# K transposed in pairs of chunks, w_down on the attention rows, masks on VectorE: a decode block on one core

## The chip, the cores and the metric

One core of one Trainium2 chip. The metric is the device time of one execution in microseconds (us); smaller is better. The profile's engines are named in full here: TensorE (PE, its weight loads PEld), VectorE (DVE), ScalarE (ACT), GpSimd (POOL), and SP, which issues most of the DMAs.

## What is computed

One decode step of a transformer block for one token, in bfloat16: a layer norm, grouped-query attention over a cache of 65,536 positions (32 query heads, 4 KV heads, width 128), the residual, a second layer norm, and a GeGLU feed-forward of width 3584 with its residual.

```python
h  = x + A(layernorm(x))            # x: [1, 1, 1024]
h2 = h + B(layernorm(h))

A: q = x @ wq                       # wq [1024, 4096], 8 query heads share a KV head
   p = softmax((q . k) * 128**-0.5) # k_cache, v_cache [4, 65536, 128]
   o = p @ v;  o @ wo               # wo [4096, 1024]
B: (gelu(x @ w_gate) * (x @ w_up)) @ w_down   # [1024, 3584] twice, [3584, 1024]
```

K and V are 67 MB each, wq and wo 8.4 MB each, the three feed-forward matrices 7.3 MB each: 173 MB that are read once.

## The kernel before

**The ring.** All large loads go through one SBUF ring of four slots of 4 MB (32 KB a partition), handed out in order by `chunk`; a load takes one or two slots, and SP issues it once the work on what lay there is done. SP's order is wq (2 slots), then K and V, wo, w_gate, w_up, w_down. The K loads are 4 MB each, two chunks of 64 positions a partition; there are 8 chunks and 4 such loads to a KV head. V of the first KV head comes in loads of 4, 4 and 8 MB, later ones in loads of 8 MB. In the first KV head K loads follow one another; from the second on, two K loads alternate with V of the head before.

**Scores.** `k_chunk` (L253) makes per chunk four VectorE transposes of 32x32 blocks, 128x1024 f32 words each, into `kt` (six buffers), and after each of them four matmuls of 512 columns into one score bank of three (L268). `score_chunk` transposes the bank back (L278) and takes maxima (L279). The queries stand in `qs`, spread over partitions by 16 small POOL copies a KV head (L226). `softmax_head` brings the maxima together and runs the exponentials on ScalarE.

**Values.** `v_chunk` multiplies with V in four column quadrants of TensorE into `acc` (L317). After a head ScalarE copies `acc` to SBUF (L326), four f32 matmuls with `sel` pick out each head's own columns (L329), and VectorE copies them into `o_raw` (L331). At the end the heads are divided by their sums and transposed (L349 to L372).

**After the attention.** wo (L410) puts the attention output on two rows of each half of `at_ps`, which `fold_columns` (L418, L420) turns into columns; VectorE adds x (L427), the second layer norm follows, and w_gate and w_up (L446, through L186 and L199).

**w_down.** Its last row of each partition's share is loaded early into `c_sb` by 12 small DMAs (L400). The rest comes as 4 MB (16 rows a partition), then 7, 3 and 1 rows. Each row is eight matmuls of 128 columns (L489), one for each eighth of the output, onto single partitions of two banks, `d_ps` and `d_odd`. The residual h is put there beforehand as `hb`, by eight POOL operations (L473) and eight matmuls (L475). Two casts (L510, L511) and the store (L512) end the kernel.

**Order.** The program is written in the order of the code, but a scheduler sets each engine's order ahead of time by when it takes operands to be ready, and adds the waits; an engine then runs its list in order. On VectorE the list has the eight transposes of a K load, then both of its chunks' score transposes and maxima, although `k_chunk` and `score_chunk` alternate in the code.

Of the kernel before, what the change touches and what calls it, by code (L numbers as in the profile page):

```python
# [9 lines left out]
ALU = mybir.AluOpType  # L10
# [7 lines left out]
def kernel(  # L18
# [47 lines left out]
    ktpool = ctx.enter_context(tc.tile_pool(name="ktpool", bufs=6))  # L66
# [3 lines left out]
    ps_m = ctx.enter_context(tc.tile_pool(name="ps_m", bufs=3, space=PSUM))  # L70
    ps_qk = ctx.enter_context(tc.tile_pool(name="ps_qk", bufs=3, space=PSUM))
    ps_acc = ctx.enter_context(tc.tile_pool(name="ps_acc", bufs=2, space=PSUM))
# [17 lines left out]
    wq_v = A_wq.rearrange("(p t c) n -> t p c n", t=DS, c=C4)  # L90
    assert C4 * HD == CW and DS * C4 == DC
    XU = 32
    XV = P // XU
    x_in = const.tile([XU, XV, DC], BF16, name="x_in")
    nc.scalar.dma_start(out=x_in[:], in_=A_x[0, 0].rearrange("(u v j) -> u v j", u=XU, j=DC))
    wq_tiles = []
    for t in range(DS):
# [16 lines left out]
    xsel = ktpool.tile([XU, XV, P], BF16, name="xsel", tag="kt")  # L114
    nc.gpsimd.memset(xsel[:], 0.0)
    nc.gpsimd.affine_select(out=xsel[:], in_=xsel[:], compare_op=ALU.not_equal, fill=1.0, base=0,
                            pattern=[[-1, XV], [1, P]], channel_multiplier=-XV)


    esel = const.tile([P, 4, P], BF16, name="esel")  # L120
    for q in range(4):
        for i in range(NI):
# [9 lines left out]
    sel16 = const.tile([P, 16], F32, name="sel16")  # L132
    nc.vector.tensor_tensor(out=sel16[:], in0=sel[:, 0:16], in1=sel[:, 16:32], op=ALU.add)
    o_of = const.tile([P, 8], F32, name="o_of")
    nc.vector.memset(o_of[:], 1.0)
    nc.gpsimd.affine_select(out=o_of[:], in_=o_of[:], compare_op=ALU.is_ge, fill=0.0, base=0,
                            pattern=[[-16, 8]], channel_multiplier=1)
    nc.gpsimd.affine_select(out=o_of[:], in_=o_of[:], compare_op=ALU.is_ge, fill=0.0, base=15,
                            pattern=[[16, 8]], channel_multiplier=-1)
# [34 lines left out]
    for v in range(XV):  # L174
        nc.tensor.matmul(x_ps[:], lhsT=xsel[:, v, :], rhs=x_in[:, v, :], start=(v == 0), stop=(v == XV - 1))
# [43 lines left out]
    def make_qs(g):  # L219

        qs = qspool.tile([P, 4, NS, P], BF16, name="qs", tag="qs")
        nc.gpsimd.memset(qs[:], 0.0)  # L222
        for i in range(NI):
            rows = slice(SQ * i, SQ * (i + 1))
            for s in range(NS):
                nc.gpsimd.tensor_copy(out=qs[rows, :, s, SQ * i + s:SQ * (i + 1):NS], in_=qsel[rows, :, g * rep:(g + 1) * rep])  # L226
        return qs
# [3 lines left out]
    o_raw = const.tile([P, Hq], F32, name="o_raw")  # L231
# [6 lines left out]
    def load(src, ci, name, blocks):  # L238

        si = ci  # L240
        for b in blocks:
            if si < DCH * b:
                break
            si -= DCH * b
        if si == 0:
            tv = chunk(b).rearrange("p (n d) -> p n d", d=Dh)
            nc.sync.dma_start(out=tv, in_=src[:, ci * CH:(ci + DCH * b) * CH, :])
            loaded[name] = tv
        return loaded[name][:, si * CH:(si + 1) * CH, :]

    def k_chunk(g, ci):

        st = kst.setdefault(g, {})  # L253
        if ci == 0:
            st["qs"] = make_qs(g)
            st["mx"] = small.tile([P, rep, NCH], F32, name="mx", tag="mx")
            st["sc"] = []
        k_sb = load(k_v[g], ci, "k_sb", [1] * (NCH // DCH))
        k32 = k_sb.rearrange("p n d -> p (n d)").bitcast(F32)
        W = NN * Dh // 2  # L260
        qk = ps_qk.tile([P, NN * SQ], F32, name="qk_ps", tag="qk")
        for s in range(NS):
            kt = ktpool.tile([P, W], F32, name="kt", tag="kt")
            nc.vector.transpose(out=kt[:], in_=k32[:, s * W:(s + 1) * W])  # L264
            mv = kt[:].bitcast(BF16).rearrange("p (n j b t) -> p n j b t", n=NN, j=2, t=2)
            for jt in range(4):
                J, t = divmod(jt, 2)
                nc.tensor.matmul(qk[:], lhsT=st["qs"][:, jt, s, :], rhs=mv[:, :, J, :, t],  # L268
                                 start=(s == 0 and jt == 0), stop=(s == NS - 1 and jt == 3))
        st[("qk", ci)] = qk  # L270
# [37 lines left out]
    def v_chunk(g, ci):  # L308
        st = vst[g]
        v_sb = load(v_v[g], ci, "v_sb", [1, 1, 2] if g == 0 else [2, 2])  # L310
        if ci == 0:
            st["acc"] = ps_acc.tile([P, NS * Dh], F32, name="acc_ps", tag="acc")
        acc = st["acc"]
        pt = st["pts"][ci // CPH]
        for n in range(NN):
            c = n % 4
            nc.tensor.matmul(acc[32 * c:32 * c + 32, :], lhsT=pt[:, ci % CPH, n, :, :].rearrange("p h s -> p (h s)"),  # L317
                             rhs=v_sb[:, n:CH:NN, :],
                             start=(ci == 0 and n < 4), stop=(ci == NCH - 1 and n >= NN - 4),
                             tile_position=(0, 32 * c))  # L320
        if ci == NCH - 1:
            assert NH == 2
            heads = slice(g * rep, (g + 1) * rep)
            nc.vector.tensor_tensor(out=lsum[:, heads], in0=st["lpart"][:, 0, :], in1=st["lpart"][:, 1, :], op=ALU.add)  # L324
            acc_sb = small.tile([P, NS * Dh], F32, name="acc_sb", tag="accsb")
            nc.scalar.copy(out=acc_sb[:], in_=acc[:])  # L326
            o_ps = misc([P, rep], F32, "o_ps")
            for t in range(NS):
                nc.tensor.matmul(o_ps[:], lhsT=acc_sb[:, t * Dh:(t + 1) * Dh], rhs=sel[:, t:SQ:NS],  # L329
                                 start=(t == 0), stop=(t == NS - 1))  # L330
            nc.vector.tensor_copy(out=o_raw[:, heads], in_=o_ps[:])  # L331
            vst.pop(g)

    VB = 2 * DCH
    for g in range(Hkv):
        for ci in range(NCH):
            k_chunk(g, ci)
            if ci >= 1:
                score_chunk(g, ci - 1)
            if ci == NCH - 1:  # L340
                score_chunk(g, ci)
                softmax_head(g)
            if g >= 1 and ci % VB == VB - 1:
                for vi in range(ci - VB + 1, ci + 1):
                    v_chunk(g - 1, vi)
    for ci in range(NCH):
        v_chunk(Hkv - 1, ci)
    l_ps = misc([P, Hq], F32, "l_ps")
    nc.tensor.matmul(l_ps[:], lhsT=ones_f[:], rhs=lsum[:], start=True, stop=True)  # L349
    rl = const.tile([P, Hq], F32, name="rl")  # L350
    nc.vector.reciprocal(out=rl[:], in_=l_ps[:])
    oT_all = const.tile([P, Hq], BF16, name="oT_all")
    nc.vector.tensor_tensor(out=oT_all[:], in0=o_raw[:], in1=rl[:], op=ALU.mult)


    WN = CW // D
    assert Hq % WN == 0 and Hq * OQ == P and Dh == OQ * Hq
    oh_ps = misc([Hq, Dh], BF16, "oh_ps")
    nc.tensor.transpose(out=oh_ps[:], in_=oT_all[:], identity=ident_bf[:])
    o_sb = small.tile([Hq, Dh], BF16, name="o_sb", tag="o_sb")  # L360
    nc.vector.tensor_copy(out=o_sb[:], in_=oh_ps[:])
# [44 lines left out]
    c_dma()  # L406
    for c in range(Hq):
        for s in range(DS):
            q = 2 * (c % 2) + s
            nc.tensor.matmul(at_ps[32 * q:32 * q + 32, :], lhsT=o2z[:, c, :], rhs=wv[:, c, :].rearrange("k (p s c) -> k s p c", s=DS, c=C4)[:, s],  # L410
                             start=(c < 2), stop=(c >= Hq - 2), tile_position=(0, 32 * q))
# [14 lines left out]
    h_col = const.tile([P, DC], F32, name="h_col")  # L426
    nc.vector.tensor_tensor(out=h_col[:], in0=hc_ps[:], in1=x_col[:], op=ALU.add)  # L427


    hz = xz  # L430
    layernorm_cols(h_col[:], hz[:, :, 0], "ln2")
# [11 lines left out]
    def ffn_in(wmat, name):  # L443
        banks = bank_pair(name + "_w", FW)
        wv = chunk(2)[:, 0:DC * F].rearrange("p (c n) -> p c n", c=DC)
        nc.sync.dma_start(out=wv, in_=wmat.rearrange("(p c) n -> p c n", p=P))  # L446
# [23 lines left out]
    hb = ktpool.tile([P, DC, P], F32, name="hb", tag="kt")  # L470
    nc.gpsimd.memset(hb[:], 0.0)
    for r in range(OR):
        nc.gpsimd.tensor_scalar(out=hb[:, :, orow[r]], in0=h_col[:], scalar1=o_of[:, r:r + 1], scalar2=None, op0=ALU.mult)  # L473
    for j in range(DC):
        nc.tensor.matmul(d_ps[:, j:OB:DC], lhsT=hb[:, j, :], rhs=sel16[:], start=False, stop=False, skip_group_check=True)  # L475
    d_odd = ps_acc.tile([P, OB], F32, name="d_odd", tag="acc")
    nc.vector.tensor_copy(out=d_odd[64:P, :], in_=d_ps[64:P, :])
# [6 lines left out]


# [11 lines left out]
    for f0, nr, pieces in ((0, FA, (FA,)), (P * FA, FB, (FB - 5, 3, 1))):  # L497
# [3 lines left out]
        for sz in pieces:  # L501
            nc.sync.dma_start(out=wv[:, e0:e0 + sz, :], in_=wsrc[:, e0:e0 + sz, :])
            for e in range(e0, e0 + sz):
                down(actz[:, f0 // P + e, :], wv[:, e, :])
            e0 += sz
        if f0 == 0:
            for r in range(4):
                down(cz[:, r, :], c_sb[:, r, :])
# [34 lines left out]
```

## Time and profile before

| | |
|---|---|
| median of 3 runs | 410.55 us (410.39 to 410.86) |
| span of the profiled execution | 408.8 us (its device time isn't printed apart) |
| DMA | 173.26 MB in 5144 packets, 424 GB/s over the span |
| TensorE busy | 228.8 us, 1623 matmuls and as many weight loads |
| VectorE busy | 205.1 us, of them 146.2 in L264's 128 transposes |
| ScalarE, GpSimd busy | 36.6 and 43.5 us |

The span runs from the first to the last instruction. In the rows of tenths each digit is a fortieth of the span, about 10.2 us. In a timeline a line has start, length, engine, line, operation, output and inputs, the count, and in brackets how long the engine had been idle before and what ended that. In the chain of work that ended last each line is a start, a length and what the end was waiting for in that time; "issue" is time in which nothing visible was waited for.

### The profile page before, as it was taken

The page shows a single profiled execution, that of the slowest core. Times are in us where ns is not written, and L with a number is a line of the kernel's source. Part 1 is how long each engine was busy: PE and PEld are TensorE (multiplying, and loading weights), DVE is VectorE, ACT ScalarE, POOL GpSimd, SP SyncE. Part 2 cuts the span into 40 slices and gives each one's busy share as a digit, 9 for nine tenths or more (in the row PEclk, how much of TensorE's full clock was granted, in tenths as well). Part 3 has the DMA queues.
Part 4 walks back from the last instruction along what each step waited for, and adds up shares of the span by engine and source line. Part 5 has one row for each costly group of instructions (what it writes and reads, how often), then busy time and mean ns, then how long its engine had stood idle before and what let it go on. Part 6 is the DMA issues. An engine that isn't in the chain of part 4 may idle for free.

```text
span 408.8 us, 3981 instructions
## 1 busy us (share of the span) xinstructions
PE 228.8 (56%) x1623; PEld 99.0 (24%) x1623; DVE 205.1 (50%) x263; ACT 36.6 (9%) x136; POOL 43.5 (11%) x150
## 2 busy tenths in 40 slices
PE   1337677688388367844765575576351425275045
PEld 1112222133133132311222222222120113143024
DVE  2118999999299239905980696089500001012010
ACT  1000000070000520000008000000340000000000
POOL 8123000300000400000002400000400100002000
PEclk9966989988888668868996689669885656566688
DMA  8999999999999999999999999999999999999995
GB/s 359 410 462 406 442 430 418 449 415 452 417 457 430 402 444 458 423 410 428 472 417 420 418 478 394 428 462 430 436 418 449 430 442 425 427 432 423 416 410 212
DMA packets 5144, 173.26 MB, mean 424 GB/s; under 512 B 643, under 2 KB 647, under 8 KB 1031
## 3 DMA queue, kind: packets, MB, share of 16 engines
q1 hardware_dynamic: 5079, 173.02, 98.4%
q8 instruction: 12, 0.20, 0.2%
q14 instruction: 5, 0.04, 0.0%
q10 hardware_dynamic: 48, 0.00, 0.0%
HBM read 173.02 MB, written 0.00 MB: 423 GB/s over the span
## 4 chain that ended last, share of the span: by engine, by line
DMA 68%; DVE 22%; PE 5%; issue 4%; SPq 0%; ACT 0%
DMA ring<-in_A_k_cache_dram 42%; DVE kt L264 19%; DMA ring<-in_A_wo_dram 8%; DMA ring<-in_B_w_up_dram 7%; DMA ring<-in_A_v_cache_dram 7%; DMA ring<-in_B_w_down_dram 4%; PE qk_ps L268 2%; PE at_ps L410 2%; PE acc_ps L317 1%; DVE sc L278 1%; DVE mx L279 1%; SPq L100 0%; PE mxT_ps L286 0%; PE d_ps L489 0%; DVE gm L288 0%
## 5 line engine op out<-in xcount | busy, mean ns | idle before, releaser
L268 PE MATMUL qk_ps<-kt,qs 128*128 128x512 bf16 x512 | 141.0, 426 | 59.8 <-DVE kt L264 46.2
L264 DVE STREAM_TRANSPOSE kt<-ring 128x1024 f32<-128x1024 f32 x128 | 146.2, 1208 | 45.4 <-DMA ring<-in_A_k_cache_dram 45.4
L268 PEld LDWEIGHTS <-qs 128*128 128x128 bf16 x512 | 53.7, 105 | 143.8 <-issue 95.1
L317 PE MATMUL acc_ps<-ring,pt 128*32 128x512 bf16 x512 | 44.7, 526 | 50.6 <-DMA ring<-in_A_v_cache_dram 50.6
L301 ACT ACTIVATE pt<-sc,nbias 128x256 bf16<-128x256 f32 x64 | 31.5, 494 | 261.9 <-DVE nbias L294 261.9
L317 PEld LDWEIGHTS <-pt 128*32 128x32 bf16 x512 | 18.4, 127 | 75.2 <-issue 51.8
L331 DVE COPY o_raw<-o_ps 128x8 f32<-128x8 f32 x4 | 0.7, 167 | 48.1 <-PE o_ps L329 48.1
L278 DVE STREAM_TRANSPOSE sc<-qk_ps 128x512 f32<-128x512 f32 x32 | 22.1, 692 | 1.0 <-PE qk_ps L268 1.0
L279 DVE TENSOR_REDUCE mx<-sc 128x8 f32<-128x512 f32 x32 | 22.0, 688 | 1.1
L222 POOL MEMSET qs<- 128x2048 bf16 x4 | 7.2, 1802 | 94.8 <-PE qk_ps L268 94.8
L186 PEld LDWEIGHTS <-xz 128*32 128x32 bf16 x192 | 6.8, 124 | 33.0 <-issue 16.1
L226 POOL COPY qs<-qsel 32x32 bf16<-32x32 bf16 x64 | 11.2, 247 | 16.6 <-DVE qsel L217 15.9
L324 DVE TENSOR_TENSOR lsum<-lpart 128x8 f32<-128x8 f32 x4 | 0.7, 164 | 24.2 <-ACT pt L301 24.2
L186 PE MATMUL qw_ps<-ring,xz 128*32 128x512 bf16 x64 | 7.2, 625 | 9.4 <-DMA ring<-in_A_wq_dram 9.4
L410 PE MATMUL at_ps<-ring,o2z 128*32 128x512 bf16 x64 | 6.6, 594 | 10.4 <-DMA ring<-in_A_wo_dram 10.4
L301 ACT ACTIVATION_READ_ACCUMULATOR pt<-sc,nbias 128x1 f32 x64 | 12.0, 187 | 0.0
L186 PE MATMUL u_ps_w<-ring,xz 128*32 128x512 bf16 (+1 forms) x64 | 4.5, 450 | 10.7 <-DMA ring<-in_B_w_up_dram 10.7
L427 DVE TENSOR_TENSOR h_col<-hc_ps,x_col 128x8 f32<-128x8 f32 x1 | 0.2, 166 | 19.5 <-PE hc_ps L420 19.5
L199 DVE STREAM_TRANSPOSE u_ps_r<-u_ps_w 128x512 f32<-128x512 f32 (+1 forms) x2 | 1.2, 629 | 14.1 <-PE u_ps_w L186 14.1
L199 DVE STREAM_TRANSPOSE q_r<-qw_ps 128x512 f32<-128x512 f32 x2 | 1.3, 696 | 13.6 <-PE qw_ps L186 13.6
L489 PE MATMUL d_ps<-ring,actz 128*32 128x128 bf16 x108 | 5.0, 263 | 5.6 <-DMA ring<-in_B_w_down_dram 5.5
L380 POOL MEMSET cz<- 128x256 bf16 x1 | 0.3, 311 | 72.6 <-PE qk_ps L268 72.6
(104 smaller groups left out, 92.0 us busy)
## 6 DMA issues: line engine op xcount, KB each, us to landing
ring<-in_A_k_cache_dram SPq DMA_DIRECT2D x16, 4096.0 KB
ring<-in_A_wq_dram SPq DMA_DIRECT2D x2, 4096.0 KB
ring<-in_A_v_cache_dram SPq DMA_DIRECT2D x2, 4096.0 KB
ring<-in_B_w_gate_dram SPq DMA_DIRECT2D x1, 7168.0 KB
ring<-in_B_w_up_dram SPq DMA_DIRECT2D x1, 7168.0 KB
ring<-in_B_w_down_dram SPq DMA_DIRECT2D x1, 4096.0 KB
ring<-in_B_w_down_dram SPq DMA_DIRECT2D x1, 1792.0 KB
ring<-in_B_w_down_dram SPq DMA_DIRECT2D x1, 768.0 KB
```

What stands on the lines that cost most here:

```text
L186: nc.tensor.matmul(banks[t // 4][32 * q:32 * q + 32, :], lhsT=rows_z[:, ci, :], rhs=w, start=first, stop=last, tile_position=(0, 32 * q))
L199: nc.vector.transpose(out=r[:, o:o + n].rearrange("p (e j) -> p e j", j=32) if sizes else r[:, o:o + n], in_=src)
L222: nc.gpsimd.memset(qs[:], 0.0)
L226: nc.gpsimd.tensor_copy(out=qs[rows, :, s, SQ * i + s:SQ * (i + 1):NS], in_=qsel[rows, :, g * rep:(g + 1) * rep])
L264: nc.vector.transpose(out=kt[:], in_=k32[:, s * W:(s + 1) * W])
L268: nc.tensor.matmul(qk[:], lhsT=st["qs"][:, jt, s, :], rhs=mv[:, :, J, :, t], start=(s == 0 and jt == 0), stop=(s == NS - 1 and jt == 3))
L278: nc.vector.transpose(out=sc.rearrange("p n h s -> p (n h s)"), in_=qk[:])
L279: nc.vector.tensor_reduce(out=st["mx"][:, :, ci], in_=sc.rearrange("p n h s -> p h n s"), axis=AX.XY, op=ALU.max)
L301: nc.scalar.activation(out=pt[:].rearrange("p c n h s -> p (c n) h s")[:, :, r, :], in_=sc[:].rearrange("p c n h s -> p (c n) h s")[:, :, ...
L317: nc.tensor.matmul(acc[32 * c:32 * c + 32, :], lhsT=pt[:, ci % CPH, n, :, :].rearrange("p h s -> p (h s)"), rhs=v_sb[:, n:CH:NN, :], start ...
L410: nc.tensor.matmul(at_ps[32 * q:32 * q + 32, :], lhsT=o2z[:, c, :], rhs=wv[:, c, :].rearrange("k (p s c) -> k s p c", s=DS, c=C4)[:, s], s ...
L489: nc.tensor.matmul((d_ps, d_odd)[q // 2][32 * q:32 * q + 32, :], lhsT=a_row[:, AZ - m:AZ - m + 32], rhs=w_row[:, j * OB:(j + 1) * OB], sta ...
```

## The change

- **K in pairs.** `k_pair` replaces `k_chunk`: four transposes of 128x2048 words cover both chunks of a load; after each, eight matmuls alternate between the two chunks' score banks, two consecutive ones with the same weights. `kt` has three buffers of twice the size. A chunk's positions are laid out accordingly in `v_chunk`. The score banks stay three.
- **Queries.** Four larger POOL copies a KV head in place of 16.
- **Heads.** After a KV head VectorE multiplies `acc` by a mask `smask` into SBUF, and one f32 matmul of 512 columns with `hsel` adds the result into an `o_ps` bank that is kept for all heads (one bank is taken from the small results). `o_raw`, its copies and the transpose at the end go; a reduction and a scaling remain.
- **x and the layouts.** x is loaded as two rows and turned into columns by four matmuls; wq, w_gate and w_up are read with a matching order of rows (w_gate and w_up as two runs a partition). The output columns of wo are read in plain order.
- **Residual.** Two matmuls put x on the attention rows of `at_ps` before wo; the add of L427 and all of `hb` go.
- **w_down.** `at_ps` is kept. Block 0, the c rows and the first piece of block 1 (now 6 rows; then 4 and 1) are two matmuls of 512 columns a row, onto the same rows of `at_ps`. Then `fold_rows` copies `at_ps` on ScalarE and adds it with eight f32 matmuls of 128 columns into `d_ps` and `d_odd`. The last five rows go as before.

```diff
...
-    ktpool = ctx.enter_context(tc.tile_pool(name="ktpool", bufs=6))
+    ktpool = ctx.enter_context(tc.tile_pool(name="ktpool", bufs=3))
...
-    ps_m = ctx.enter_context(tc.tile_pool(name="ps_m", bufs=3, space=PSUM))
+    ps_m = ctx.enter_context(tc.tile_pool(name="ps_m", bufs=2, space=PSUM))
     ps_qk = ctx.enter_context(tc.tile_pool(name="ps_qk", bufs=3, space=PSUM))
+    ps_o = ctx.enter_context(tc.tile_pool(name="ps_o", bufs=1, space=PSUM))
...
-            for s in range(NS):
-                nc.gpsimd.tensor_copy(out=qs[rows, :, s, SQ * i + s:SQ * (i + 1):NS], in_=qsel[rows, :, g * rep:(g + 1) * rep])
+            nc.gpsimd.tensor_copy(out=qd[rows, :, :, SQ * i:SQ * (i + 1):NS],
+                                  in_=qsel[rows, :, g * rep:(g + 1) * rep].unsqueeze(2).to_broadcast([SQ, 4, NS, rep]))
...
-        W = NN * Dh // 2
-        qk = ps_qk.tile([P, NN * SQ], F32, name="qk_ps", tag="qk")
+        W = DCH * NN * Dh // 2
+        qks = [ps_qk.tile([P, NN * SQ], F32, name="qk_ps", tag="qk") for _ in range(DCH)]
         for s in range(NS):
             kt = ktpool.tile([P, W], F32, name="kt", tag="kt")
             nc.vector.transpose(out=kt[:], in_=k32[:, s * W:(s + 1) * W])
...
             for jt in range(4):
                 J, t = divmod(jt, 2)
-                nc.tensor.matmul(qk[:], lhsT=st["qs"][:, jt, s, :], rhs=mv[:, :, J, :, t],
-                                 start=(s == 0 and jt == 0), stop=(s == NS - 1 and jt == 3))
+                for c in range(DCH):
+                    nc.tensor.matmul(qks[c][:], lhsT=st["qs"][:, jt, s * P:(s + 1) * P], rhs=mv[:, c, :, J, :, t],
+                                     start=(s == 0 and jt == 0), stop=(s == NS - 1 and jt == 3))
...
-            nc.scalar.copy(out=acc_sb[:], in_=acc[:])
...
+            nc.vector.tensor_tensor(out=acc_sb[:], in0=acc[:].rearrange("p (s d) -> p s d", d=Dh),
+                                    in1=smask[:].unsqueeze(2).to_broadcast([P, NS, Dh]), op=ALU.mult)
+            nc.tensor.matmul(o_ps[:], lhsT=hsel[:, Hq - rep - g * rep:2 * Hq - rep - g * rep],
+                             rhs=acc_sb[:].rearrange("p s d -> p (s d)"), start=(g == 0), stop=(g == Hkv - 1))
...
-        for ci in range(NCH):
-            k_chunk(g, ci)
-            if ci >= 1:
-                score_chunk(g, ci - 1)
...
+        for cp in range(NCP):
+            k_pair(g, cp)
+            if cp >= 1:
+                for ci in range((cp - 1) * DCH, cp * DCH):
+                    score_chunk(g, ci)
...
+    for s in range(DS):
+        nc.tensor.matmul(at_ps[32 * s:32 * s + 32, :], lhsT=ident_bf[0:DS, s:s + 32], rhs=x_in[:], start=True, stop=False,
+                         tile_position=(0, 32 * s))
...
-        nc.sync.dma_start(out=wv, in_=wmat.rearrange("(p c) n -> p c n", p=P))
+        nc.sync.dma_start(out=wv.rearrange("p (s c) n -> p s c n", s=DS), in_=wmat.rearrange("(s p c) n -> p s c n", s=DS, c=C4))
...
-    hb = ktpool.tile([P, DC, P], F32, name="hb", tag="kt")
-    nc.gpsimd.memset(hb[:], 0.0)
...
+    fz = qspool.tile([P, DS, 2 * AZ + 1], F32, name="fz", tag="qs")
+    nc.gpsimd.memset(fz[:], 0.0)
+    nc.gpsimd.tensor_copy(out=fz[:, :, AZ], in_=sel2[:])
+
+    def down_wide(a_row, w_row, i):
+        for s in range(DS):
+            q = 2 * (i % 2) + s
+            nc.tensor.matmul(at_ps[32 * q:32 * q + 32, :], lhsT=a_row[:, AZ:AZ + 32], rhs=w_row[:, s * NB:(s + 1) * NB],
+                             start=False, stop=False, skip_group_check=True, tile_position=(0, 32 * q))
+
+    def fold_rows():
+        r = ktpool.tile([P, NB], F32, name="d_w", tag="kt")
+        nc.scalar.copy(out=r[:], in_=at_ps[:])
+        for j in (0, 4, 1, 5, 2, 6, 3, 7):
+            q, m = divmod(orow[j], 32)
+            s, b = divmod(j, OR // DS)
+            nc.tensor.matmul((d_ps, d_odd)[q // 2][32 * q:32 * q + 32, :], lhsT=fz[:, s, AZ - m:AZ - m + 32], rhs=r[:, b * OB:(b + 1) * OB],
+                             start=False, stop=False, skip_group_check=True, tile_position=(0, 32 * q))
...
-    for f0, nr, pieces in ((0, FA, (FA,)), (P * FA, FB, (FB - 5, 3, 1))):
+    for f0, nr, pieces in ((0, FA, (FA,)), (P * FA, FB, (FB - 6, 4, 1))):
...
+                if i == 0:
+                    down_wide(actz[:, f0 // P + e, :], wv[:, e, :], e)
+                else:
+                    down(actz[:, f0 // P + e, :], wv[:, e, :])
...
+            elif i == 0:
+                fold_rows()
...
```

## The prediction

> **What bounds the kernel now.** I read the slices of the span first, then the DMA queues, the chain that ended last, and the timelines of SP, VectorE and TensorE around the places where the chain touches DMA.
>
> ```profile
> DVE  2118999999299239905980696089500001012010
> ...
> DMA  8999999999999999999999999999999999999995
> GB/s 359 410 462 406 442 430 418 449 415 452 417 457 430 402 444 458 423 410 428 472 417 420 418 478 394 428 462 430 436 418 449 430 442 425 427 432 423 416 410 212
> ...
> q1 hardware_dynamic: 5079, 173.02, 98.4%
> q8 instruction: 12, 0.20, 0.2%
> ...
> DMA 68%; DVE 22%; PE 5%; issue 4%; SPq 0%; ACT 0%
> ```
>
> The reader is to see that the DMA row is full from the second slice to the last but one, and that one queue accounts for 98.4% of the 16 engines' span. The chain's 22% of VectorE look like a second bound, but during them DMA is full too: the chain follows a slot that was freed early. The packet records of the trace say it more sharply: a 32,768-byte packet takes 1213 ns on its engine from the first weight load to the last K load, 16 engines x 27.0 GB/s = 432 GB/s, and the next packet starts as the last ends. So what matters is (1) whether the queue ever runs dry, (2) the bytes and packets, (3) what follows the last landing.
>
> For (1), SP's timeline and VectorE's:
>
> ```profile
> 101.17 0.33 SPq L247 DMA_DIRECT2D ring<-in_A_k_cache_dram  x1
> 105.99 0.33 SPq L247 DMA_DIRECT2D ring<-in_A_v_cache_dram  x1
> ```
>
> ```profile
> 92.02 9.12 DVE L264 STREAM_TRANSPOSE kt<-ring 128x1024 f32<-128x1024 f32 x8
> ...
> 111.41 1.25 DVE L264 STREAM_TRANSPOSE kt<-ring 128x1024 f32<-128x1024 f32 x1 [7.56 <-DMA ring<-in_A_k_cache_dram]
> ```
>
> The load at 101.17 waits for the sixth pair's eight transposes (92.02 + 9.12) and is wanted when the load before it has landed: its engines finish it between 109.5 and 111.25, VectorE sees it at 111.41. That is 8 to 10 us early, the least reserve in the attention; the others have 8.1 us (issue at 287.88) to 19.5 us.
>
> For (3), the chain's end:
>
> ```profile
> 389.20 16.87 DMA ring<-in_B_w_down_dram
> 406.06 0.04 issue
> 406.11 0.23 PE d_ps L489 x2
> ...
> 406.48 0.26 ACT h L511
> ```
>
> From 406.06 to 408.8, 2.7 us, there are eight matmuls, two casts and the store; the change touches none of them.
>
> **The sum, part by part.** It is made against the span of the profiled execution, 408.8; the median of the runs, 410.55, lies 1.75 above, and I carry that over.
>
> *K two chunks at a time.* A pair had 8 transposes of 1024 at 1.14 (9.12 in all), then two score transposes and maxima, 2.6: 11.7 a pair (32.29, 43.99, 55.69). It will have 4 of 2048. The 1024s fix no overhead; between no saving (2.28 each) and one tenth of a us each I take 2.21, 8.84 a pair. Against that, both chunks now end with the last transpose: eight matmuls must follow it, at 0.216 each at full clock 1.7 us, where four did (0.9) and the first chunk's scores hid them. If VectorE stands still for that, a pair takes 8.84 + 1.75 + 2.6 = 13.2. It need not: the order on VectorE is fixed ahead by the scheduler, which takes what is ready; at 80.00 it put a transpose between two steps of the softmax. Three score banks let the next pair begin once the first score transpose is through, so the second chunk's 1.3 us can fill the gap: 11.9 to 12.6. Over five periods this puts the sixth pair's end at 41.1 + 5 x 12.3 + 1.25 (softmax steps) = 103.9 instead of 101.17; the reserve hides it. Cost 0; without the cover, see the second rival. Loads, ring and their order stay.
>
> At the row where the granted clock stands (0.50 from 57.3 to 60.8 us, just after TensorE idled 2.79) a rule speaks against this change. The Trainium skill, TensorE: Matmul & The Clock Gate, section "Why this matters for your kernels", asks for no TensorE gaps beyond about 3 us. The new gap is 2.6 + 2.2 = 4.8 us; by the rule each pair starts at half clock, and a pair without filler takes 13.4 instead of 13.2.
>
> *Masks, head extraction, x.* Per KV head an ACT copy (0.59), eight f32 passes (1.06) and a copy (0.17) become one VectorE multiply (between the 0.16 of a tiny one and the 0.72 of a 512-column PSUM transpose, nearest the latter) and one matmul of 512 f32 columns (two passes). The multiply waits for the head's last V matmuls; behind it on VectorE stand the next pair's transposes, which wait for their load anyway (the copy it replaces ended at 148.79, that load came at 150.16); after the last head the chain to o2z ended at 345.4, 9.7 before wo landed at 355.1. Query spreading on POOL goes from 16 copies of 0.247 to 4 larger ones (each 0.25 to 1), beside the load that lands at 32.2; the first transpose needs no query. Hidden: 0. x comes in two packets instead of 32; it landed at 6.8 and the layer norm was done 0.6 before wq at 12.9. The x matmuls into the attention rows wait for nothing late. Keeping those rows in their bank leaves two score banks for w_up, free when w_gate's rows are transposed at 377.7, 11 before w_up lands. The dropped h_col add (0.17) and hb work (2.3 on POOL, 2.0 on TensorE) had over 3 us before w_gate and 12 before w_down: 0.
>
> *Weight layouts.* wq keeps 32,768-byte packets. w_gate and w_up go from 57,344 (2120 ns) to two of half that; by the line through 32,768 (1213) and 65,536 (2422) a half takes 1062, so +4 ns x 8 packets x 2 loads = +0.07 us on each engine. w_down's pieces 14,336 + 6,144 (538 + 234) become 12,288 + 8,192, 772 by the same line: 0.
>
> *w_down.* It has to be done before the last 256 KB land. Block 0 landed at 399.34, TensorE at clock 0.50 until 402.3. Now 32 matmuls of 512 in four quadrants: L410's 64 took 6.58 at half clock, so 3.2 to 402.55, and the four c rows at full clock 0.43: 403.0, as before. Six rows land at 403.63 - 1/7 of 4.29 = 403.0: 12 matmuls 0.65, drain 0.2, ACT copy 0.59 (L418), fold from 404.6. The fold is 8 matmuls of 128 f32 columns, 16 passes:
>
> ```profile
> 376.52 1.96 PE L475 MATMUL d_ps<-sel,hb 128*128 128x16 f32 x16
> ```
>
> ```profile
> 362.42 2.03 PE L420 MATMUL hc_ps<-sel,at_r 128*128 128x2 f32 x8 [0.69 <-ACT at_r L418]
> ```
>
> Here 16 passes took 1.96 with 128 weight columns; the fold loads 32 and spreads over quadrants, where L489's bf16 ones run at 0.014 each. So 0.2 to 2.0, at half clock (second line) up to 4; between, I take 1.0, half of L475, since pairs of quadrants run together. Then four rows, landed at 405.6, 32 matmuls in 0.45: done at 406.1, as the last piece lands at 406.1. Delay 0 to 0.2 around this, I take 0.1. The fold's first matmul is the added wait: behind it stand the last five rows' 40 matmuls and then both casts. Its weights are made on POOL in a slot that may be free only after the c rows, 403.0: a memset (0.53 for 512 columns, L383) and a copy (0.25) end at 403.8, still before 404.6. The Trainium skill, Perfetto Trace Analysis, section "Engine Utilization", halves the output rate for FP32_LOW_HIGH; as an estimate 16 x 128 columns at half rate are 1.7 us in one quadrant row, 0.85 in two, close to what I took.
>
> *Instructions.* 179 fewer matmuls, 24 o_ps, 16 hb and 140 w_down passes above all, and 64 fewer transposes. Fetches share the engines: at 40.52 a 16,384-byte packet held one engine and its next data packet, together 1.5 us longer than that data packet alone. They come every 256 or so TensorE instructions, 12 in the span. The engines end their last piece between 402.4 and 405.9, and the last has two fetches (87.8, 376.7). Later fetches go away (403.9) or move, those two stay: 0.
>
> Sum: 0.07 + 0.1 = +0.2, 410.55 + 0.2 = **410.7**, with 410.2 to 411.3 for this case.
>
> **Rivals.**
> - *The fold is late.* For: TensorE takes its work in order, so the last five rows queue behind the copy and the passes. Against: L489's overlap. With L475's 1.96 the rows end at 407.0, 0.9 late: 411.5; at L420's rate (16 passes 4.1) 414. It decides from a fold of 1.1 us on and passes 0.2% at 1.8. Slower; chance 0.15.
> - *VectorE falls behind in the first KV head.* If nothing fills the gap, a pair takes 13.2; with its first eight matmuls at half clock 2.2 + 3.4 + 3 x 1.7 + 2.6 = 13.4, with the first sixteen 15. The sixth pair ends at 41.1 + 5T + 1.25: 108.4 at 13.2, 117.4 at 15. A load needs 1.1 to 1.3 from issue to first packet (0.79 to 2.13; 406.81 to 407.9), the first engine is dry at 109.5. It decides at T = 13.2: at 13.4 it costs 0.8 (411.5), at 15 some 9 (419.5). Against: slots are filled, above. Chance 0.12.
> - *Fewer fetches.* If the shared weights of a chunk pair are loaded once, 256 instructions more go and the fetch at 376.7 comes after its engine's end: the next engine ends 0.2 earlier; if others lose theirs too (POOL's at 33.3, VectorE's at 394.1) the bound is the mean of the 16 ends, 404.3, 1.6 earlier: 409.0 to 410.4. Against: every matmul here has its own weight load (512 and 512). Chance 0.11.
> - That the edits do little for their engines is part of the forecast: 3% of the transposes' time, on an engine that waits for loads.
>
> **How the numbers follow.** Forecast 0.62, rivals 0.15, 0.12, 0.11. Within 0.2% (0.8 us, about what a measurement of this kernel can tell from no change): the forecast, 0.04 of the fetch case and 0.03 from the low edges of the others, 0.69; slower 0.13 + 0.11 = 0.24; faster 0.07, the better part of the fetch case. The range 409.9 to 412.0 takes in the rest of the fetch case and most of the late fold, and leaves out the dry queue, the slowest fold and the case that the engines come out even, about 0.18 in all.
>
> **What would show it.** Right: DMA row full, packets of 1213 ns, 2.7 to 2.9 us from last landing to end, the eighth K load issued before 108. Wrong: an idle DMA slice near 110, TensorE busy with the fold when the last piece lands, or last landings spread less than 3.5 us.

## The result

The changed kernel takes 412.71 us (median of 5 runs, 412.19 to 412.94) beside 410.67 us (410.39 to 410.86) of the kernel before in the same comparison: a ratio of 1.0047, with a 95% interval of 1.0036 to 1.0058. It is slower by 2.0 us, and above the predicted range. The profiled execution has a span of 410.4 us and a device time of 412.19, against a span of 408.8.

**The page.** These are the lines of the page of after that answer to those of before, with the row of the granted clock between them:

```profile
DVE  3018777977999536924782787087600002011010
...
PEclk9965787678998787687986698767858858565567
DMA  8999999999999999989998999999999999999994
...
q1 hardware_dynamic: 5335, 173.02, 98.2%
q8 instruction: 11, 0.18, 0.2%
...
DMA 56%; PE 22%; DVE 16%; issue 3%; ACT 2%; SPq 0%; ACTq 0%
```

The DMA row has two 8s (slices 18 and 22, 174 to 226 us) where before had only 9s, but they are not the loss: the packet records show all 16 engines at work there. What was lost lies in slice 11, near 110 us, and is too short to lower its digit. In the chain TensorE has risen from 5% to 22%. VectorE's slices 5 to 10, all 9 before, are now 7 but for one: it does less, and it stands still in between. One group of after tells for what:

```profile
L257 DVE STREAM_TRANSPOSE kt<-ring 128x2048 f32<-128x2048 f32 x64 | 142.3, 2278 | 30.6 <-DMA ring<-in_A_k_cache_dram 30.6
...
L273 DVE STREAM_TRANSPOSE sc<-qk_ps 128x512 f32<-128x512 f32 x32 | 21.1, 696 | 34.3 <-PE qk_ps L262 34.3
```

Ahead of its score transposes VectorE is idle for 34.3 us in all, and TensorE's matmuls end that time. The same line of before:

```profile
L278 DVE STREAM_TRANSPOSE sc<-qk_ps 128x512 f32<-128x512 f32 x32 | 22.1, 692 | 1.0 <-PE qk_ps L268 1.0
```

**The pairs.** VectorE's timeline of after, for the third and fourth pair of the first KV head:

```profile
59.13 8.85 DVE L257 STREAM_TRANSPOSE kt<-ring 128x2048 f32<-128x2048 f32 x4
67.90 1.24 DVE L274 TENSOR_REDUCE mx<-sc 128x8 f32<-128x512 f32 x2
71.24 1.31 DVE L273 STREAM_TRANSPOSE sc<-qk_ps 128x512 f32<-128x512 f32 x2 [2.10 <-PE qk_ps L262]
72.47 0.65 DVE L274 TENSOR_REDUCE mx<-sc 128x8 f32<-128x512 f32 x1
73.04 8.88 DVE L257 STREAM_TRANSPOSE kt<-ring 128x2048 f32<-128x2048 f32 x4
81.84 0.65 DVE L274 TENSOR_REDUCE mx<-sc 128x8 f32<-128x512 f32 x1
85.03 1.31 DVE L273 STREAM_TRANSPOSE sc<-qk_ps 128x512 f32<-128x512 f32 x2 [2.55 <-PE qk_ps L262]
```

Four transposes take 8.85 us, as they should. But both score transposes (one of them ahead of the sixth pair) stand ahead of the next pair's first transpose, and only the maxima of the pair before are left for the time in which the last eight matmuls run. So VectorE stands still for 2.1 to 3.0 us in each of the first five pairs. The pairs begin at 32.37, 46.02, 59.13, 73.04, 87.42 and 100.21: 13.57 us apart on the mean, where the same five periods of before, softmax steps included, took 11.95 (32.29 to 92.02). TensorE's timeline of after, in the same stretch:

```profile
48.38 9.69 PE L262 MATMUL qk_ps<-kt,qs 128*128 128x512 bf16 x32 [3.98 <-DVE kt L257]
61.45 9.97 PE L262 MATMUL qk_ps<-kt,qs 128*128 128x512 bf16 x32 [3.38 <-DVE kt L257]
75.39 9.82 PE L262 MATMUL qk_ps<-kt,qs 128*128 128x512 bf16 x32 [3.97 <-DVE kt L257]
...
106.92 1.90 PE L262 MATMUL qk_ps<-kt,qs 128*128 128x512 bf16 x8 [0.30 <-DVE kt L257]
```

Between two pairs TensorE is idle for 3.4 to 4.6 us, and its 32 matmuls then take 9.7 to 10.0 us. In the sixth pair, at full clock, eight of them take 1.90 (last line), and the 32, with a transpose to wait for every 2.2 us, 8.5. The granted clock over each stretch (the third column from the right) was this in after:

```profile
44.00:56.00 12.00, 8.02 (x26) 2.87 (x25) 11.25 (x8) 0.00 (x0) 0.00 (x0) 0.72 1.00 431
56.00:68.00 12.00, 8.62 (x28) 3.08 (x27) 10.11 (x7) 0.00 (x0) 0.00 (x0) 0.72 0.98 423
68.00:80.00 12.00, 8.03 (x27) 2.97 (x26) 9.90 (x9) 0.00 (x0) 0.00 (x0) 0.75 1.00 429
```

and this in before, whose gaps between pairs are 2.79 us:

```profile
44.00:56.00 12.00, 8.24 (x32) 3.06 (x33) 11.93 (x14) 0.00 (x0) 0.00 (x0) 1.00 0.99 426
56.00:68.00 12.00, 8.91 (x32) 3.45 (x32) 11.93 (x13) 0.00 (x0) 0.00 (x0) 0.86 0.99 427
```

**The load.** SP's line for the eighth K load (101.17 in before), and two stretches of after by engine, in which the last two columns are the DMA share and GB/s:

```profile
109.09 0.33 SPq L239 DMA_DIRECT2D ring<-in_A_k_cache_dram  x1
```

```profile
108.00:110.00 2.00, 1.70 (x9) 0.68 (x8) 2.00 (x3) 0.00 (x0) 0.00 (x0) 1.00 0.57 246
110.00:112.00 2.00, 2.00 (x25) 0.83 (x27) 2.00 (x5) 0.00 (x0) 0.00 (x0) 1.00 1.11 360
```

The load is issued 7.9 us later than before, and the queue runs dry. In the packet records the engines finish the load before it from 109.04 on, and the first new packet starts at 110.05, 0.96 us after the issue. The 16 engines are idle for 0.55 us each on the mean. Then 14 of the 16 first packets take 1672 to 2055 ns instead of 1213, another 0.55 on the mean. The seventh load, issued at 96.77 and 2.6 us ahead of the first engine's end, had lost 0.17 on the mean already: four of its packets took 1508 to 2273 ns. The last engine is done with the eighth load 1.4 us late (122.01 for 120.64), and with the last piece of w_down 1.45 late (407.07 for 405.62). Nothing takes it back on the way, since the queue is full from there on. (These are times on the axis of the timelines. The prediction's packet times stand 0.31 us later than that axis: its 109.5, 111.25 and 405.9 are 109.2, 110.9 and 405.6 here.)

**The end.** After, from w_down's block 0 on:

```profile
400.78 3.60 PE L477 MATMUL at_ps<-ring,actz 128*32 128x512 bf16 x32 [3.23 <-DMA ring<-in_B_w_down_dram]
...
406.04 0.59 ACT L482 COPY d_w<-at_ps 128x512 f32<-128x512 f32 x1 [25.60 <-PE at_ps L477]
...
406.77 0.30 PE L486 MATMUL d_ps<-d_w,fz 128*32 128x128 f32 x2 [0.83 <-ACT d_w L482]
...
407.20 0.25 PE L492 MATMUL d_ps<-ring,actz 128*32 128x128 bf16 x2
...
407.99 0.28 DVE L518 CAST h<-d_ps 64x128 bf16<-64x128 f32 x1 [10.23 <-PE d_odd L492]
```

The 16 passes of the fold take 0.43 us up to the start of the next row (406.77 to 407.20), and the casts come 0.92 after the end of the last packet, where before they came 0.82 after it (406.44 and 405.62). So of the 1.6 us by which the span grew, 1.45 are the late loads and 0.1 the end.

### The profile page after: what moved, and what is told of

It reads as the page before. It is cut to its first block, busy times and chain, and to the rows that moved or that the text cites. A ratio compares the mean times of both kernels' runs of the same rounds, so it can differ in the third digit from the quotient of the medians.

```text
span 410.4 us, 3480 instructions
## 1 busy us (share of the span) xinstructions
PE 233.5 (57%) x1444; PEld 96.3 (23%) x1444; DVE 199.6 (49%) x199; ACT 34.8 (8%) x133; POOL 36.1 (9%) x91
## 4 chain that ended last, share of the span: by engine, by line
DMA 56%; PE 22%; DVE 16%; issue 3%; ACT 2%; SPq 0%; ACTq 0%
DMA ring<-in_A_k_cache_dram 36%; PE qk_ps L262 16%; DVE kt L257 12%; DMA ring<-in_B_w_gate_dram 8%; DMA ring<-in_B_w_down_dram 6%; DMA ring<-in_A_v_cache_dram 6%; PE acc_ps L312 3%; DVE sc L273 2%; ACT pt L296 2%; DVE mx L274 2%; PE at_ps L477 1%; PE g_ps_w L176 1%; PE bc_ps L287 0%; SPq L99 0%; PE mxT_ps L281 0%
## 5 line engine op out<-in xcount | busy, mean ns | idle before, releaser
L262 PE MATMUL qk_ps<-kt,qs 128*128 128x512 bf16 x512 | 146.9, 451 | 66.7 <-DVE kt L257 66.7
L257 DVE STREAM_TRANSPOSE kt<-ring 128x2048 f32<-128x2048 f32 x64 | 142.3, 2278 | 30.6 <-DMA ring<-in_A_k_cache_dram 30.6
L262 PEld LDWEIGHTS <-qs 128*128 128x128 bf16 x512 | 56.3, 110 | 153.1 <-issue 106.2
L312 PE MATMUL acc_ps<-ring,pt 128*32 128x512 bf16 x512 | 42.0, 500 | 27.0 <-DMA ring<-in_A_v_cache_dram 24.0
L273 DVE STREAM_TRANSPOSE sc<-qk_ps 128x512 f32<-128x512 f32 x32 | 21.1, 696 | 34.3 <-PE qk_ps L262 34.3
L274 DVE TENSOR_REDUCE mx<-sc 128x8 f32<-128x512 f32 x32 | 20.3, 653 | 0.0
L320 DVE TENSOR_TENSOR acc_sb<-acc_ps,smask 128x512 f32<-128x512 f32 x4 | 2.7, 687 | 33.9 <-PE acc_ps L312 33.9
L212 POOL MEMSET qs<- 128x2064 bf16 x4 | 7.2, 1812 | 100.6 <-PE qk_ps L262 100.6
L216 POOL COPY qs<-qsel 32x128 bf16<-32x128 bf16 x16 | 7.9, 491 | 19.5 <-DVE qsel L207 18.8
L176 PE MATMUL g_ps_w<-ring,xz 128*32 128x512 bf16 (+1 forms) x64 | 5.8, 553 | 5.8 <-DMA ring<-in_B_w_gate_dram 5.8
L322 PE MATMUL o_ps<-acc_sb,hsel 128*32 128x512 f32 x8 | 5.0, 718 | 6.8 <-DVE acc_sb L320 6.8
```

The lines of the kernel that those rows point to most:

```text
L176: nc.tensor.matmul(banks[t // 4][32 * q:32 * q + 32, :], lhsT=rows_z[:, ci, :], rhs=w, start=first, stop=last, tile_position=(0, 32 * q))
L216: nc.gpsimd.tensor_copy(out=qd[rows, :, :, SQ * i:SQ * (i + 1):NS], in_=qsel[rows, :, g * rep:(g + 1) * rep].unsqueeze(2).to_broadcast([SQ ...
L262: nc.tensor.matmul(qks[c][:], lhsT=st["qs"][:, jt, s * P:(s + 1) * P], rhs=mv[:, c, :, J, :, t], start=(s == 0 and jt == 0), stop=(s == NS ...
L273: nc.vector.transpose(out=sc.rearrange("p n h s -> p (n h s)"), in_=qk[:])
L274: nc.vector.tensor_reduce(out=st["mx"][:, :, ci], in_=sc.rearrange("p n h s -> p h n s"), axis=AX.XY, op=ALU.max)
L322: nc.tensor.matmul(o_ps[:], lhsT=hsel[:, Hq - rep - g * rep:2 * Hq - rep - g * rep], rhs=acc_sb[:].rearrange("p s d -> p (s d)"), start=(g ...
```

## The experiments

**The theory after the result:** the pairs make VectorE free the ring slots too late; the eighth K load is issued when the queue is running dry; all of the loss comes from there. **The rivals:** the fold or the wide rows at the end (they work for K in any form), or the new layouts.

**K chunk by chunk again** (with six `kt` buffers, as in before), the rest as changed.

```diff
-        for cp in range(NCP):
-            k_pair(g, cp)
+        for ci in range(NCH):
+            k_chunk(g, ci)
```

> The changed kernel with K transposed and multiplied chunk by chunk as before (six buffers of 1024), all else as changed. Dry queue (VectorE falls behind in the first KV head and the eighth K load is issued at 109.08): the issue goes back to about 101 and the time to 410.7 to 411.1, that is 410.67 plus 0.1 to 0.3 for the layouts and the fold. Late fold: nothing of the tail changes, so 412.5 to 412.8. Layouts or instruction fetches: 412 to 412.7.

410.51 us (11 runs), a ratio of 0.9998 (0.999 to 1.0007). The load goes out at 101.22, no engine is idle. So the fold, the wide rows, the masks and the layouts together cost nothing that can be measured in the median, and without the pairs there is no loss.

**The pairs alone, in the kernel before.**

> The kernel before with K in pairs and nothing else of the change. Dry queue: eighth K load issued at 108.5 to 109.5, DMA engines idle near 110, 411.9 to 412.7. Late fold, layouts or fetches: 410.5 to 410.8, since none of them is in it.

411.84 us, 1.003 (1.0014 to 1.0046), and with a spread that neither kernel has: 410.64 to 414.67. The profiled execution was one of the short ones: its load went out at 104.49, no engine was idle, the span was 408.9. The list of its 11 runs shows what they differ in. The four with a mean granted clock of 0.770 and more have spans of 408.8 to 409.4; the seven with 0.759 and less have 409.6 to 412.7. In the kernel before the clock varies as well (0.766 to 0.808), with spans of 408.7 to 409.1. So the pairs bring the load close to the edge. That the clock decides on which side it falls fits the two traces: this kernel's first pairs had a granted clock of 0.86 to 1.00 and VectorE's waits were 0.6 to 2.4 us, after's had 0.70 to 0.75 and 2.1 to 3.0. The runs alone don't show it, since their clock is a mean over the whole execution. The five runs of after all lay at 0.759 to 0.771, with spans of 410.4 to 411.2. The Trainium skill, TensorE: Matmul & The Clock Gate, in "What's actually happening", says that the window by which the clock is set runs freely, so that one kernel warms up at different places from run to run; these eleven runs, with mean clocks of 0.744 to 0.789, agree with that.

**The fold first.** The changed kernel with `fold_rows` ahead of w_down, all of whose rows then go as eighths.

> The changed kernel with the attention rows folded before the first w_down row and every w_down row as eighths, so that no fold stands in the tail. Dry queue: the tail gives back 0.1 to 0.3 only, 412.3 to 412.7. Late fold: 410.7 to 411.1.

412.58 us (nine runs, 411.45 to 416.21), 1.0061 (1.0038 to 1.0083), and the profiled load went out at 107.56. The last packet of w_down ended at 407.18, 1.56 late, so the late loads are there without a fold at the end, as they were gone with the fold in place in the first experiment. So the late fold isn't their cause. The rest of this kernel's span of 411.5 is its own end: its last rows ran at half clock (0.52 from 407.0 to 409.5), and the casts came 1.9 us after the last packet instead of 0.8. Here the mean clock doesn't sort the runs: one at 0.763 has a span of 410.6, one at 0.789 has 413.2.

**The last matmuls chunk by chunk.** After the fourth transpose of a pair the first chunk's four matmuls run before the second's, so that its scores are done after four.

```diff
+            order = [(jt, c) for jt in range(4) for c in range(DCH)]
+            if s == NS - 1:
+                order.sort(key=lambda o: o[1])
-            for jt in range(4):
...
-                for c in range(DCH):
+            for jt, c in order:
```

> The changed kernel with one order of matmuls changed: after the fourth transpose of a pair the first chunk's four matmuls come before the second chunk's four, so that its scores start 0.9 us (1.7 at half clock) earlier. Dry queue: a pair takes 11.7 to 12.6 instead of 13.4, the eighth K load is issued before 106, no engine is idle near 110, 410.7 to 411.2. Late fold, layouts or fetches: 412.5 to 412.8.

410.73 us, 1.0006 (0.9997 to 1.0015). VectorE's waits fall to 0.5 to 2.0, and the load goes out at 106.06 (before 106 was expected). Two of the 11 runs, those with the lowest clock (0.759 and 0.767), still have spans of 410.0 and 410.1; the rest have 408.6 to 409.3. Four matmuls that come earlier are enough, but barely.

**VectorE's time by itself: spare transposes in the kernel before.** Nobody reads them. One, seven in six pairs, and two a pair, in the first six pairs:

```diff
+        if ci % DCH == 0 and g * NCH + ci < 12:
+            spare = ktpool.tile([P, W], F32, name="spare", tag="kt")
+            nc.vector.transpose(out=spare[:], in_=k32[:, 0:W])
```

> The kernel before with one spare transpose of 128x1024 (1.14 us, its result unused) in each of the first six pairs, 6.8 us in all: the eighth K load is issued at about 108.0 instead of 101.17. Dry queue with the first engine empty at 109.5 and 1.1 to 1.3 from issue to first packet: 0 to 0.4, 410.6 to 411.1. If more VectorE work as such cost time, or its reads of the ring slowed the loads: 412 to 417.

> As the one before, with a second spare transpose in the sixth pair, 8.0 us in all: issue at about 109.1, as in the changed kernel. Dry queue: 411.6 to 412.6, the changed kernel's loss without any other part of the change. Otherwise as the one before.

> Two spare transposes in each of the first six pairs, 13.7 us in all: issue at about 114.9, 5.8 later than in the changed kernel. Dry queue: about 5.8 more than with seven spares, 417 to 418.5. If the scheduler fills waits with them: less, in step with the issue.

Measured: 411.67 (1.0018 to 1.0046), 411.98 (1.0027 to 1.0047) and 415.66 us (1.0113 to 1.0139). Work on VectorE alone, with every other part as before, gives a loss of the same kind and, with the load issued as late as in after, of nearly the same size. The issues of the eighth K load in the three:

```profile
106.96 0.33 SPq L247 DMA_DIRECT2D ring<-in_A_k_cache_dram  x1
```

```profile
108.76 0.33 SPq L247 DMA_DIRECT2D ring<-in_A_k_cache_dram  x1
```

The third kernel's seventh and eighth load stand in one line, the eighth ending with it: 99.17 + 13.97 - 0.33 = 112.81.

```profile
99.17 13.97 SPq L247 DMA_DIRECT2D ring<-in_A_k_cache_dram  x2
```

Two of the three came out of their range. The third lost less because 13.7 us of spares moved its load by 11.6 only: the scheduler set score transposes between the K transposes. Its loss is one of the queue and not of VectorE's work as such: the seventh load (issued at 99.17) left the engines idle for 0.7 us on the mean, the eighth for 3.1, the long packets after each cost 0.55, and these sum to 4.9, as much as the last packet of w_down was late (410.49 for 405.62). The first kernel lost more than expected, and that was to be learned from. Profiled executions side by side, from the packet records (the first of the 16 engines is done with the load before at 109.04 to 109.17, in the last kernel at 110.40; long packets are counted for 4 us from there):

| kernel | issue | idle from there on, mean of 16 | packets over 1300 ns | last engine done | span |
|---|---|---|---|---|---|
| before | 101.17 | 0 | 0 | 120.64 | 408.8 |
| pairs alone | 104.49 | 0 | 0 | 120.59 | 408.9 |
| last by chunk | 106.06 | 0 | 0 | 120.96 | 408.9 |
| one spare | 106.96 | 0.12 | 6 | 122.66 | 410.5 |
| fold first | 107.56 | 0.37 | 20 | 121.18 | 411.5 |
| seven spares | 108.76 | 0.57 | 15 | 121.64 | 410.1 |
| after | 109.09 | 0.55 | 15 | 122.01 | 410.4 |
| two spares | 112.81 | 3.1 | 16 | 125.47 | 413.7 |

With one spare a single engine was idle, for 2.0 us (109.18 to 111.16), and six packets took 1339 to 2432 ns. One engine lost so much that the last eight of w_down's 128 last packets, 0.08 apart, ended at 406.71 to 407.27, when the other 120 had ended by 405.62. So in these executions the loss begins between 106.1 and 107.0, 2.2 to 3.0 us ahead of the first engine's end, and not at the 0.96 that pass from the issue to the first packet. Near the edge it falls in some executions only: three of the seven runs with one spare took 410.9 to 411.1 us, the others 411.7 to 412.9. Past that point the time isn't a plain function of the issue, since it is the worst engine that counts.

**The order on VectorE, by hand.** In the changed kernel the next pair's first transpose now runs ahead of the two score transposes, within a KV head.

```diff
+            if s == 1 and cp >= 1:
+                for ci in range((cp - 1) * DCH, cp * DCH):
+                    score_chunk(g, ci, kt0, kt)
...
+        nc.vector.tensor_copy(out=scf[:, 0:1], in_=kt0[:, 0:1])
         nc.vector.transpose(out=scf, in_=qk[:])
+        nc.vector.tensor_copy(out=kt1[:, 0:1], in_=scf[:, 0:1])
```

The copies hold the order; a transpose then overwrites what they wrote.

> The changed kernel, with VectorE's order set by hand: within a KV head the next pair's first transpose runs ahead of the two score transposes of this pair, and the other three after them (eight copies of one column per pair boundary, about 0.06 us each, hold the order). The time between two KV heads stays as it was. Theory (the loss comes from VectorE standing still for the pair's last matmuls, 2.1 to 2.96 us a pair, because both score transposes stand ahead of the next pair): the transpose of 2.2 us covers the wait, a pair takes 8.85 + 1.3 + 1.2 + 0.3 = 11.7 to 12.2, the eighth K load is issued between 101 and 105 instead of 109.08, no first packet is slow, no lane is idle near 110: 410.4 to 410.9, the time before. Rival (pairs of chunks cost by themselves, by 128x2048 transposes or by the shared banks, whatever the order): the period stays near 13.6 and the time near 412.7.

410.57 us (410.31 to 411.47), 1.0 (0.999 to 1.0009). VectorE's timeline of this kernel (the line at 48.72 holds the last three transposes of the second pair and the first of the third, the line at 60.40 the same one pair later):

```profile
48.72 8.88 DVE L261 STREAM_TRANSPOSE kt<-ring 128x2048 f32<-128x2048 f32 x4
57.63 0.22 DVE L279 COPY sc<-kt 128x1 f32<-128x1 f32 x2
57.89 1.31 DVE L280 STREAM_TRANSPOSE sc<-qk_ps 128x512 f32<-128x512 f32 x2
...
60.40 8.88 DVE L261 STREAM_TRANSPOSE kt<-ring 128x2048 f32<-128x2048 f32 x4
```

The wait is gone within a KV head, and a pair takes 60.40 - 48.72 = 11.68 us, as in before. SP issues the load at 103.20. The profiled execution, with a span of 409.4, is one of the longer ones; its last packet ended at 405.46, so its loads weren't late. So pairs of 128x2048 are no dearer than single chunks; where the scores stand is what costs.

**The gap filled.** The changed kernel, VectorE's order as it was, with spare matmuls in TensorE's gap:

```diff
+        if g * NCP + cp < 5:
+            warm = misc([P, NN * SQ], F32, "warm")
+            for _ in range(12):
+                nc.tensor.matmul(warm[:], lhsT=st["qs"][:, 0, 0:P], rhs=mv[:, 0, :, 0, :, 0], start=True, stop=True)
```

> The changed kernel with 12 spare matmuls of 512 columns after each of the first five pairs, whose result nobody reads; they fill 2.6 of the 3.4 to 4.6 us in which TensorE stands still between two pairs. VectorE's order stays. Theory (the gaps cost the clock: of a pair's 9.7 us of matmuls the first part runs at half clock, the granted clock is 0.74 to 0.80 over a pair, and the last eight matmuls therefore come late): with the clock at 1.0 the last eight take 1.9, VectorE waits 1.3 to 1.8 instead of 2.1 to 2.96, a pair takes 12.4 to 12.8, the eighth K load is issued between 103.5 and 105.5 and the time is 410.4 to 410.9. Rival (the clock follows something else, or the order alone sets the wait): the granted clock stays below 0.85 in the pairs, the spare matmuls take 0.43 each, 5.2 us, and hold up the next pair: issue at 109 or later, 412.5 to 415.

410.86 us, 1.0004 (0.9995 to 1.0013). The granted clock, then TensorE and VectorE in this kernel:

```profile
46.00:59.00 13.00, 10.53 (x46) 4.22 (x45) 11.80 (x9) 0.00 (x0) 0.00 (x0) 1.00 1.01 436
59.00:73.00 14.00, 10.62 (x46) 4.40 (x46) 12.80 (x10) 0.00 (x0) 0.00 (x0) 1.00 1.03 442
```

```profile
56.00 2.76 PE L267 MATMUL warm<-kt,qs 128*128 128x512 bf16 x12
60.13 1.90 PE L262 MATMUL qk_ps<-kt,qs 128*128 128x512 bf16 x8 [1.37 <-DVE kt L257]
```

```profile
68.43 1.31 DVE L277 STREAM_TRANSPOSE sc<-qk_ps 128x512 f32<-128x512 f32 x2 [1.20 <-PE qk_ps L262]
```

The gap is 1.37 us, the clock stays at 1.00 in these pairs (0.72 to 0.75 in after), VectorE waits 1.20 there instead of 2.1 to 3.0, a pair takes 12.45 (12.74 on the mean of the five periods) and the load goes out at 104.86. Sixty matmuls that nobody needs undo the loss as far as it can be measured. So the wait has two parts: eight matmuls at full clock, which the order exposes, and the half clock, which the gap brings. The second part is what carries the load over the edge.

No kernel here is faster than before. Those that lose nothing end at the same 410.5 to 410.9, because their queue never runs dry and they read the same bytes.

## Why the prediction was wrong

- **The failed step** is the cover on VectorE in the pair's period: "the second chunk's 1.3 us can fill the gap: 11.9 to 12.6". Three banks do allow it, and with the order set by hand it happens (11.68). But it was taken for what the scheduler would do, from one transpose that stood between two softmax steps at 80.00 in before. In after it put both score transposes ahead of the next pair, and left only one or two maxima to fill: 13.57 on the mean of five periods instead of 12.55 (12.3 and a fifth of the 1.25 for the softmax steps), and the load at 109.09 instead of 103.9. So the reserve, which was to hide the delay at a cost of 0, was used up.
- **The rival "VectorE falls behind in the first KV head"** is what happened, with the half clock that it named. It had a chance of 0.12. Its first figure was 13.4 (its terms add up to 13.3), and the measured mean without the softmax steps is 13.3. Its threshold of 13.2 was too high: the loss begins at an issue between 106.1 and 107.0, which by its own formula are 12.7 to 12.9.
- **Its price was too low.** From issue to first packet 0.96 us passed; the 1.1 to 1.3 are 0.8 to 1.0 on the axis of the timelines, and the dry engine's 109.5 moves by the same 0.31, so this did no harm. That the first packets after a dry queue are long (0.55 on the mean) wasn't in it, although the kernel before shows it at its own start: the packets that start from 1.82 to 1.95 us took 1801 to 2127 ns, so the 1213 didn't hold from the first load on. Nor was it in it that the loss begins 2.2 to 3.0 us ahead of the dry engine. The 0.8 us became 1.45, and the median of the runs lies another 0.5 above the profiled one.
- **The rule on the clock held** (the Trainium skill, TensorE: Matmul & The Clock Gate, "Why this matters for your kernels", as the prediction told it): after gaps of 3.4 to 4.6 us each pair began at half clock, after 1.37 at full clock; gaps of 2.6 to 3.1 (before, and the kernel with the order set by hand) did either, with stretches at 0.76 to 1.00. Half clock followed gaps of 2.79 and 2.95 us too, so about 3 us was no safe line here. The estimate of 4.8 for the gap was somewhat high. That the clock cost "13.4 instead of 13.2" wasn't near: 12.74 against 13.57 on the mean of five periods, 0.8 us a pair.
- **The transposes**: 8.84 forecast, 8.85 to 8.89 measured. **Masks, x, query spreading, layouts** at 0.1 us in all: not contradicted by the kernel with K chunk by chunk, whose interval of 0.999 to 1.0007 can't resolve 0.1.
- **The fold**: the start at 404.6 was met to the tenth where the landing wasn't late (K chunk by chunk: 404.60). It takes 0.43 to 0.65 instead of 1.0, and delays nothing that can be measured in the median. Where the wide rows ran at half clock to the end it does cost: in after the copy came at 406.04, which is the 0.1 us of the end, and in the profiled execution of the kernel with the order set by hand at 405.00, and the casts came 1.5 us after the last packet instead of 0.8. So the rival "The fold is late" was at work there, with 0.7 us, in single executions.
- **Fewer fetches**: 11 on the page instead of 12, and no gain; the kernels without the loss stand at the time of before.

## What to carry to other kernels

When two chunks end together, look at what the engine behind them has left to do in the meantime, in the order that the scheduler really sets, and not in the best one that the buffers allow. A reserve of 8 us in front of a full queue was spent here by 1.6 us a step over five steps; count it in steps, and put the edge some 3 us ahead of the dry queue, where these executions had it. An idle gap on an engine off the critical path is no harmless thing if its clock falls in it: filling it with useless work was worth 0.4% here (412.71 to 410.86 us).

## What the runs showed of the hardware that was not expected

- After a dry queue the first packet of nearly every engine is long: 1672 to 2055 ns instead of 1213 in after, 1415 to 2112 in the kernel with two spares.
- A load that is issued 2.2 us before the first engine is done can already cost: with one spare transpose a pair one engine was idle for 2.0 us, single packets took up to 2432 ns, and the time rose by 0.3%. At 3.0 us (the last matmuls chunk by chunk) none did.
- A delay of one engine stays with it to the end: in that kernel the last eight packets of w_down, 0.08 us apart, ended 1.1 to 1.65 us after the other 120, 290 us later.
- Sixteen f32 passes with 32 weight columns in four quadrants took 0.43 us up to the next row's start, where sixteen with 128 columns took 1.96.

What stays open: why all five runs of after fell on the side of the low clock, and only seven of 11 of the kernel with the pairs alone, whose pairs have the same transposes and matmuls, so that it loses 1.2 us in the median where after loses 2.0. It may be chance, or what came before the first pair; no run here separates the two.
